# A conformer block on one core: chunk transposes by VectorE and DMA, and part of the exponentials' products on GpSimd

## Chip, cores and metric

The kernel runs on one core of a Trainium2 chip. The metric is the device time of one execution in microseconds (us); shorter is better. The engines are named as in the profile: PE (TensorE), PEld (its weight loads), DVE (VectorE), ACT (ScalarE), POOL (GpSimd) and SP (SyncE, which here issues transfers).

## What is computed

One conformer block on x of 2 x 4000 tokens with 144 features, in bfloat16: half a feed-forward layer, attention with 4 heads of 36 features over all 4000 tokens of a sequence, a gated convolution of width 5 over time, half a feed-forward layer, and a layer norm. Cut to what matters:

```python
h = layernorm(x); x = x + 0.5 * (silu(h @ w_ff1a) @ w_ff1b)
q, k, v = split(layernorm(x) @ w_qkv)
p = softmax(q @ k.T * Dh ** -0.5)            # per head: 4000 x 4000 scores
x = x + (p @ v) @ w_o
a, b = split(layernorm(x) @ w_pw1); h = a * sigmoid(b)
x = x + silu(depthwise_conv5(h, dw)) @ w_pw2
h = layernorm(x); x = x + 0.5 * (silu(h @ w_ff2a) @ w_ff2b)
return layernorm(x)
```

## The kernel before

**Chunks and score tiles.** The 8000 tokens are 16 chunks of 500 (8 a sequence), each kept as 4 blocks of 125 tokens, one token per partition. For attention, the keys of a sequence are 62 tiles of 64 and one of 32, so there are 16 x 63 = 1008 score tiles: 64 keys by 500 queries by 4 heads, as 128 partitions by 1000 columns. A tile is made by `emit_S` (L1357): four matmuls on quarters of PE's array into two PSUM banks. Its exponential goes into a slot of PT, of which there are 11, and `emit_O` (L1439) multiplies it with V by four more quarter matmuls into two banks that a chunk keeps for itself.

**Two ways to an exponential.** ACT's way (`emit_exp`, L1371) is one instruction of 1000 columns. DVE's way (`dve_tile`, L1385) has five. Two read the scores from PSUM, one per bank, and write them as 16-bit integers to a slot z. The third takes z's mantissa bits into a second slot y. The fourth (L1409) multiplies z with y into y, and the fifth keeps of z the exponent bits alone, in place. Then both y and z are multiplied with V, so a DVE tile costs PE a second product. The function `due` (L1611) says when a tile takes DVE's way; it takes 167 of the 1008 so.

**Around attention.** A chunk's normalised rows have to lie with features on partitions before a matmul can take them. `ln` (L704) does the norm: the statistics on DVE, the power -1/2 on POOL, and the rows by POOL (L724), or in the first and the last part of the kernel by DVE or ACT. `transp` (L693) then transposes the chunk: for each half of 72 features and each of the 4 blocks one PE transpose against an identity into a bank, 8 in all, and one copy of 1000 columns from PSUM to XT or XTQ. This is done five times for a chunk: ahead of the first feed-forward layer, ahead of the projections to Q, K and V (into XTQ, `ln_trq`, L756), for the attention's result AN (`post1`, L1089, written by `epilogue`, L1292), for the norm behind it, and ahead of the second feed-forward layer (`post2`, L1214). The matmuls that read XT or XTQ (`mm2`, L783, `ff_tile`, L793, `proj`, L882, `glu`, L1022) take two halves of 72 features each.

**Order of the work.** All instructions of an engine run in one order that a planner writes when the kernel is built. `Rec.op` (L71) keeps for each engine the time at which it comes free, by a cost for each instruction; `Sched` (L259) holds threads of work (`pre`, `post1`, `post2` for a chunk), and `pick_any` (L1524) chooses the next step among score tiles, exponentials, products with V and threads. A table POLICY (L373) gives 49 sections of the kernel their own parameters, AHEAD for one: how far ahead of ACT PE is to be kept. Where an instruction needs another engine's result, it waits on that engine's semaphore, and whatever stands behind it on its own engine waits too. The phase in which the first 8 chunks are prepared is called front, the one after the last exponential tail. In these two a chunk is handled in halves of two blocks.

**Start.** L568 to L597 issue the loads of x and the weights (SP and ACT) and the zeroings (POOL and DVE). DVE makes IDF, a 32-bit copy of the identity, there (L597), ahead of the first chunk's statistics.

Of the kernel before, what the change touches and what calls it, by code (L numbers as in the profile page):

```python
# [12 lines left out]
D = 144  # L13
# [29 lines left out]
def c_act(n):  # L43
    return n / 1200 + 0.051
# [6 lines left out]
class Rec:  # L51
# [6 lines left out]
    SWITCH = 0.095  # L58
# [12 lines left out]
    def op(self, eng, name, *a, r=(), w=(), q=None, cost=0.1, kind=None, lat=None, **k):  # L71
# [29 lines left out]
        if eng == "pe":  # L101
            if kind != self.kind:
                start += self.SWITCH
            self.kind = kind
# [4 lines left out]
        self.ops.append(o)  # L109
        return o  # L110
# [141 lines left out]
class Thread:  # L252
    def __init__(self, gen, ready, rank, no=0):
        self.no = no
        self.gen, self.ready, self.live, self.rank = gen, ready, True, rank
        self.req = None
# [67 lines left out]
def bass_standalone__conformer_family_zipformer__speech_kernel(  # L324
# [28 lines left out]
    def sb(name, shape, dt=BF16):  # L353
# [5 lines left out]
    NAN = 5  # L359
    TJ = (  # L360
        0.0, -0.6, 0, 0.0, -0.3, 0.0, 0.0, 0.0, 0.0, -0.6, 0.15, 0.15, -0.6, 0.0, 0.15, 0,
        0.0, 0.0, 0.0, 0.0, 0.0, 0.0, 0.3, 0.6, 0.6, -0.3, -0.3, 0.0, 0.0, 0.0, 0.0, 0.0,
        0.0, 0.0, 0.0, 0.15, 0.0, 0.0, 0.0, -0.15, 0.0, 0.0, 0.0, 0.0, 0, 0.6, 0.0, 0.0,
    )
    FJ = (
        0.0, 0.0, 0.0, 0.0, 0.0, 0.0, 0.0, 0.0, 0.0, 0.0, 0.0, 0.0, 0.0, 0.0, 0.0, 0.0,
        0.0, 0.0, 0.0, 0.0, 0.0, 0.0, 0.0, 0.0, 0.0, 0.0, 0.0, 0.0, 0, 0.0, 0.0, 0.0,
        -0.25, 0.0, 0.0, 0.0, 0.0, 0.0, 0.0, 0.0, 0.0, 0.0, 0, 0.0, 0.0, 0.0, 0.0, 0.0,
        0.0, 0.0, 0.0, 0.0, 0.0, 0.0, 0.0, 0.0, 0.0, 0.0, 0.0, 0.0, 0.0, 0.0, 0.0, 0.0,
    )  # L370
    FLEX = 0.3
    SEG = 21
    POLICY = {  # L373
        "AHEAD": (
            0.56, 0.56, 0.56, 0.85, 0.85, 0.85, 0.56, 0.56, 0.56, 0.56, 0.56, 0.56, 1.0, 1.0, 0.56, 0.56,
            0.56, 0.56, 0.56, 0.56, 0.56, 0.56, 0.56, 0.56, 0.56, 0.6, 0.6, 0.5, 0.5, 0.5, 0.5, 0.56,
            0.56, 0.56, 0.56, 0.56, 0.56, 0.56, 0.56, 0.56, 0.5, 0.5, 0.56, 0.56, 0.56, 0.56, 0.56, 0.56,
            0.56,
        ),
        "DSLACK": (  # L380
            0.4, 0.4, 0.4, 2.5, 1.5, 1.5, 1.5, 1.0, 1.0, 1.5, 0.8, 0.4, 0.4, 0.4, 0.2, 0.2,
            0.4, 0.4, 0.4, 0.4, 1.5, 1.5, 1.5, 1.5, 4.0, 4.0, 4.0, 0.4, 0.4, 0.2, 0.4, 0.4,
            0.4, 0.4, 0.4, 0.4, 0.4, 0.4, 0.2, 0.2, 0.2, 0.4, 0.4, 0.4, 0.4, 1.5, 1.5, 1.5,
            1.5,
        ),
        "DGAP": (
            2.0, 2.0, 4.0, 3.5, 4.5, 4.5, 4.5, 2.5, 2.5, 2.5, 2.5, 2.5, 2.5, 2.5, 2.5, 2.5,
            2.5, 2.5, 2.5, 2.5, 4.5, 2.5, 2.5, 2.5, 2.5, 2.5, 3.0, 3.25, 3.25, 3.0, 6.0, 3.25,
            3.25, 3.25, 3.25, 3.25, 4.0, 2.5, 2.5, 2.5, 3.25, 3.25, 3.25, 4.5, 4.5, 4.5, 3.25, 3.25,
            3.25,  # L390
        ),
        "OFREE": (
            3, 3, 1, 1, 4, 4, 1, 1, 1, 3, 0, 0, 0, 0, 1, 1,
            1, 1, 1, 1, 1, 1, 1, 1, 1, 1, 1, 2, 1, 1, 1, 1,
            1, 1, 1, 1, 1, 1, 0, 0, 0, 0, 0, 1, 2, 0, 0, 1,
            1,
        ),
        "OBATCH": (
            1, 1, 2, 1, 1, 1, 1, 1, 1, 1, 1, 1, 1, 1, 1, 1,
            1, 1, 1, 1, 1, 1, 1, 1, 0, 2, 2, 2, 2, 2, 2, 1,  # L400
            1, 1, 1, 1, 1, 1, 2, 1, 1, 1, 1, 1, 1, 1, 3, 2,
# [3 lines left out]
            0.3, 0.3, 0.3, 0.3, 0.6, 0.6, 0.1, 0.2, 0.2, 0.2, 0.2, 0.2, 0.6, 0.6, 0.6, 0.1,  # L405
            0.1, 0.1, 0.1, 0.1, 0.1, 0.3, 0.3, 0.3, 0.3, 0.3, 0.2, 0.2, 0.2, 0.3, 0.3, 0.3,
            0.3, 0.3, 0.2, 0.2, 0.2, 0.2, 0.2, 0.2, 0.2, 0.2, 0.2, 0.2, 0.2, 0.2, 0.2, 0.2,
# [3 lines left out]
            1.8, 1.8, 1.6, 1.6, 1.6, 1.6, 1.6, 2.0, 2.5, 2.5, 2.5, 2.5, 2.5, 1.4, 2.5, 2.5,  # L411
            2.5, 1.8, 2.5, 2.5, 2.5, 1.6, 1.6, 1.6, 1.6, 1.6, 1.6, 1.4, 1.4, 1.4, 1.4, 3.5,
            3.5, 3.5, 3.5, 2.5, 2.5, 1.4, 1.4, 1.4, 1.6, 1.6, 3.0, 3.0, 1.4, 1.4, 1.4, 1.8,
# [3 lines left out]
            2, 2, 2, 2, 2, 2, 2, 2, 2, 3, 3, 3, 3, 3, 2, 2,  # L417
            5, 5, 4, 2, 2, 3, 2, 2, 2, 2, 2, 2, 2, 4, 2, 4,
            4, 5, 5, 2, 2, 2, 4, 5, 5, 5, 5, 5, 5, 5, 5, 4,
# [3 lines left out]
            3, 3, 2, 2, 1, 1, 1, 1, 1, 2, 2, 2, 2, 3, 3, 3,  # L423
            3, 2, 2, 2, 2, 3, 3, 2, 2, 1, 1, 2, 2, 3, 3, 3,
            3, 3, 3, 3, 3, 3, 2, 3, 3, 4, 3, 3, 3, 3, 3, 3,
            3,
        ),
        "MAXQ": (
            2, 2, 3, 3, 1, 1, 3, 2, 1, 1, 1, 1, 1, 1, 3, 2,
            3, 3, 2, 2, 1, 2, 2, 2, 2, 1, 1, 2, 2, 2, 2, 2,  # L430
            2, 2, 2, 2, 2, 2, 3, 1, 1, 1, 3, 3, 3, 3, 3, 3,
            3,
        ),
        "EARLY": (
            2, 2, 2, 1, 3, 3, 2, 2, 2, 2, 2, 2, 2, 1, 1, 1,
            2, 2, 1, 1, 2, 2, 2, 2, 2, 2, 2, 2, 2, 2, 2, 2,
            2, 1, 1, 2, 2, 2, 3, 3, 3, 3, 3, 3, 2, 2, 2, 2,
# [3 lines left out]
            0.12, 0.12, 0.12, 0.12, 0.05, 0.05, 0.3, 0.12, 0.12, 0.05, 0.05, 0.05, 0.05, 0.05, 0.12, 0.12,  # L441
            0.12, 0.12, 0.12, 0.12, 0.12, 0.12, 0.12, 0.12, 0.12, 0.12, 0.12, 0.12, 0.2, 0.2, 0.2, 0.12,
            0.3, 0.2, 0.2, 0.2, 0.2, 0.2, 0.12, 0.12, 0.12, 0.12, 0.12, 0.12, 0.12, 0.12, 0.12, 0.12,
            0.12,
        ),
        "TWIN": (
            0.1, 0.1, 0.1, 0.1, 0.1, 0.1, 0.1, 0.1, 0.1, 0.1, 0.1, 0.1, 0.1, 0.1, 0.1, 0.1,
            0.1, 0.1, 0.1, 0.1, 0.1, 0.1, 0.1, 0.1, 0.0, 0.0, 0.0, 0.1, 0.1, 0.1, 0.1, 0.1,
            0.1, 0.1, 0.1, 0.1, 0.1, 0.1, 0.1, 0.1, 0.1, 0.1, 0.1, 0.1, 0.1, 0.1, 0.1, 0.1,
            0.1,  # L450
        ),
        "BGPICK": (
            0, 0, 0, 0, 0, 0, 0, 0, 0, 0, 0, 0, 0, 0, 0, 0,
            0, 0, 0, 0, 0, 0, 0, 0, 0, 0, 0, 0, 0, 0, 0, 0,
            1, 1, 1, 0, 0, 0, 1, 0, 0, 0, 0, 0, 0, 0, 0, 0,
# [3 lines left out]
            2, 2, 2, 1, 2, 2, 2, 2, 2, 0, 0, 0, 0, 0, 2, 2,  # L459
            2, 2, 2, 2, 2, 2, 2, 2, 2, 2, 2, 2, 2, 2, 0, 0,  # L460
            2, 2, 2, 2, 2, 3, 2, 2, 2, 2, 2, 2, 2, 2, 2, 2,
            2,
        ),
        "FDVE": (
            5, 5, 5, 5, 5, 5, 5, 5, 5, 5, 5, 5, 4, 4, 4, 5,
            5, 3, 3, 3, 3, 5, 5, 5, 5, 5, 5, 5, 5, 2, 2, 5,
            5, 5, 5, 5, 5, 5, 5, 5, 5, 5, 5, 5, 5, 1, 5, 5,
            5,
        ),
        "PRELAG": (  # L470
            0.7, 0.7, 0.7, 0.7, 0.7, 1.0, 0.7, 1.5, 1.5, 0.7, 0.7, 0.7, 0.7, 0.7, 0.7, 0.7,
            0.7, 0.7, 0.7, 0.7, 0.7, 0.7, 0.7, 0.7, 0.7, 0.7, 0.7, 1.0, 1.0, 1.0, 1.0, 0.7,
            0.7, 0.5, 0.5, 0.5, 0.5, 0.5, 0.7, 0.3, 0.3, 0.3, 0.7, 0.7, 0.5, 0.5, 0.5, 0.5,
            1.0,
        ),
        "LAGD": (
            1, 1, 1, 1, 1, 1, 1, 0, 0, 0, 0, 0, 1, 1, 0, 1,
            1, 1, 1, 1, 1, 1, 1, 1, 1, 1, 1, 1, 1, 0, 0, 0,
            1, 1, 1, 1, 1, 1, 1, 1, 1, 1, 1, 0, 0, 0, 0, 1,
# [19 lines left out]
    XN = sb("XN", [NXN, NB, D])  # L499
# [4 lines left out]
    XT = sb("XT", [NXT, 2, CW])  # L504
# [11 lines left out]
    AN = sb("AN", [NAN, NB, D])  # L516
# [24 lines left out]

    PS = nc.alloc_psum_tensor("PS", [128, 8 * 512], F32)
# [14 lines left out]

    def load_x(eng, c, r=()):
        load(eng, f"x{c}", X[0:TB, c * NB:(c + 1) * NB, :], x_tok[c], [("X", c, i) for i in range(NB)], r, 2.9)

    def load_ff(eng, qa, qb, WA, WE, WB, wa, wb, nm, la=None, lb=None):
        load(eng, qa, WA[0:HD, :, :], kh(wa)[:, :, 0:512], [(nm, "a", 0)], lat=la)
        load(eng, qa, WE[0:HD, :, 64:128], kh(wa)[:, :, 512:FF], [(nm, "a", 1)], lat=la)
        load(eng, qb, WB[:, 0:4, :], wb[0:512, :].rearrange("(t p) d -> p t d", p=128), [(nm, "b", 0)], lat=lb)
        load(eng, qb, WB[0:64, 4, :], wb[512:FF, :], [(nm, "b", 1)], lat=lb)
        load(eng, qb, WB[64:128, 5, :], wb[512:FF, :], [(nm, "b", 2)], lat=lb)

    load_x("sp", 0)  # L568
# [7 lines left out]
    op("pool", "memset", NHALF[:, :], -0.5, w=["NHALF"])  # L576
    op("pool", "memset", WP2Z[:, :, :], 0.0, w=[("WP2Z", i) for i in range(NB)], cost=0.3)
    op("pool", "memset", U2[:, :, :], 0.0, w=["U20"], cost=0.6)
    load("sp", "w2", WO[0:HD, :, :], kh(w_o), ["WO"])
    load("sp", "w2", WP1[0:HD, :, :], kh(w_pw1), ["WP1"])  # L580
# [9 lines left out]
    for WE, WB, nm, eng in ((WE1, WB1, "W1", "dve"), (WE2, WB2, "W2", "pool")):  # L590
        op(eng, "memset", WE[0:HD, :, 0:64], 0.0, w=[(nm, "a", 2)], cost=0.15)
        op(eng, "memset", WE[0:HD, :, 128:192], 0.0, w=[(nm, "a", 3)], cost=0.15)
# [61 lines left out]
    def setup_dw():  # L654
        for ab in range(2):
            op("dve", "tensor_copy", WPZ[0:HD, :, 48 + 64 * ab:64 + 64 * ab], WP1[0:HD, :, ab * D + ML:(ab + 1) * D],
               r=["WP1", "WPZ0"], w=["WPZ"], cost=0.15)
# [35 lines left out]
    def transp(src, rk, dst, wk, n, rows=TB):  # L693
# [830 lines left out]
    def pick_any():  # L1524
# [46 lines left out]
        if n_s[0] >= NIT and o:  # L1571
            return o[0]
# [133 lines left out]
```

## Time and profile before

| | |
|---|---|
| Median of 3 runs | 914.84 us (914.69 to 915.0) |
| The profiled execution: its own time, its span | 914.9 us, 913.1 us |
| Granted TensorE clock | 0.999 |
| Busy: PE, DVE, ACT, POOL | 890.1, 802.0, 872.9, 277.5 us |
| First exponential, last exponential start | 20.59 us, 877.89 us |
| Exponentials on ACT | 825 of 1000 columns, 16 of 500 |
| Normalisations of a block on POOL | 224, mean 599 ns |
| Transfers | 7.36 MB in 7322 packets |

The span runs from the first to the last instruction of the profiled execution; the time is a little longer. A group line gives line, engine, operation, out<-in by the program's names, shapes (partitions x elements), count, then busy time and the mean in ns of one, then the idle time of the engine just before them and who ended it. Nearly every instruction has line 170, since one helper (`replay`) issues them all, so groups are told apart by names and shapes. A line of a stretch gives, after its bounds and length, the busy time (and count) of PE, PEld, DVE, ACT and POOL, the granted clock, and the share and rate of the DMA engines. A line of the timeline gives start, duration, engine, line, operation, names and count.

### The profile page before, as it was taken

What the parts mean: (1) busy time and instruction counts of PE and PEld (TensorE: products, weight loads), DVE (VectorE), ACT (ScalarE), POOL (GpSimd) and SP (SyncE); (2) the same over time, 40 slices, a digit from 0 to 9 for tenths busy, and PEclk for the clock granted to TensorE, in tenths of its full rate; (3) what the DMA queues carried; (4) which work ended last, traced back from release to release, by engine and by line L of the source; (5) the groups of instructions that cost most, each with busy time, mean ns of one, the idle gap of its engine ahead of it and who ended that gap; (6) DMA issues with size and microseconds to landing.
All of it is one profiled execution on the core that took longest, in us unless ns stands there. A gap on an engine that the chain in (4) does not pass through costs nothing.

```text
span 913.1 us, 27439 instructions
## 1 busy us (share of the span) xinstructions
PE 890.1 (97%) x11946; PEld 411.2 (45%) x11946; DVE 802.0 (88%) x1756; ACT 872.9 (96%) x1105; POOL 277.5 (30%) x519
## 2 busy tenths in 40 slices
PE   8999999999999999999999999999999999999996
PEld 7544434444444444444444444444434344444455
DVE  8988898898989999898988799897889699978987
ACT  5899999999999999999999999999999999999984
POOL 5121041145111612223415333240605050403143
PEclk9999999999999999999999999999999999999999
DMA  4000000000000000000000000000000000000000
GB/s 114 34 2 1 2 2 1 1 3 1 3 3 1 3 2 2 2 3 1 2 2 14 1 9 8 8 2 1 15 1 2 8 9 2 8 1 8 2 8 26
DMA packets 7322, 7.36 MB, mean 8 GB/s; under 512 B 2376, under 2 KB 7202, under 8 KB 7202
## 3 DMA queue, kind: packets, MB, share of 16 engines
q1 hardware_dynamic: 5786, 5.00, 1.8%
q8 instruction: 93, 1.52, 0.7%
q10 hardware_dynamic: 1416, 0.62, 0.3%
q14 instruction: 27, 0.22, 0.1%
HBM read 3.31 MB, written 2.30 MB: 6 GB/s over the span
## 4 chain that ended last, share of the span: by engine, by line
ACT 51%; PE 43%; DVE 4%; issue 1%; DMA 0%; POOL 0%; POOLq 0%; DVEq 0%
ACT PT L170 46%; PE PS L170 43%; ACT TH L170 5%; DVE HT L170 1%; DVE PT L170 1%; DVE ST L170 1%; DMA X<-in_x_dram 0%; DVE X L170 0%; DVE XN L170 0%; DVE QT L170 0%; POOL RS L170 0%; DVE XT L170 0%; DVE RS L170 0%; DVE SW L170 0%; DVE VA L170 0%
## 5 line engine op out<-in xcount | busy, mean ns | idle before, releaser
L170 ACT ACTIVATE PT<-PS 128x1000 bf16<-128x1000 f32 (+1 forms) x841 | 777.2, 1050 | 8.3 <-PE PS L170 5.9
L170 PE MATMUL PS<-QT,KT 64*64 64x500 bf16 x3968 | 415.6, 383 | 8.6 <-ACT PT L170 5.6
L170 PE MATMUL PS<-PT,VA 64*37 64x500 bf16 x4636 | 396.1, 373 | 1.9 <-DVE QT L170 1.4
L170 DVE TENSOR_SCALAR PT<-PS 128x500 int16<-128x500 f32 x334 | 222.4, 671 | 31.5 <-PE PS L170 29.5
L170 PEld LDWEIGHTS PS<-QT,KT 64*64 64x64 bf16 x3968 | 123.8, 104 | 195.7 <-ACT PT L170 112.5
L170 PEld LDWEIGHTS PS<-PT,VA 64*37 64x37 bf16 x4636 | 132.1, 95 | 111.3 <-issue 26.7
L170 POOL TENSOR_SCALAR RS<-ST 125x4 f32<-125x4 f32 x112 | 36.6, 327 | 471.0 <-DVE ST L170 465.8
L170 DVE TENSOR_SCALAR PT<-PT 128x1000 uint16<-128x1000 uint16 x334 | 134.7, 416 | 1.3
L170 POOL TENSOR_SCALAR XN<-X,RS 125x144 bf16<-125x144 bf16 x224 | 131.8, 599 | 5.8
L170 POOL TENSOR_TENSOR RS<-RS,NHALF 125x4 f32<-125x4 f32 (+2 forms) x101 | 94.1, 936 | 101.6 <-DVE RS L170 96.9
L170 DVE TENSOR_TENSOR PT<-PT 128x1000 bf16<-128x1000 bf16 x167 | 113.0, 681 | 1.5
L170 ACT ACTIVATE TH<-PS 128x500 bf16<-128x500 f32 (+3 forms) x198 | 104.3, 552 | 6.7 <-PE PS L170 5.6
L170 DVE SCALAR_TENSOR_TENSOR HT<-TH,PS 128x500 bf16<-128x500 bf16 (+1 forms) x135 | 80.6, 616 | 25.1 <-ACT TH L170 24.4
L170 PE MATMUL PS<-XT,WA 72*128 72x500 bf16 (+2 forms) x280 | 74.3, 360 | 0.6 <-DVE VA L170 0.3
L170 DVE SCALAR_TENSOR_TENSOR X<-PS,X 125x288 bf16<-125x288 f32 x128 | 57.4, 452 | 14.8 <-PE PS L170 13.1
L170 DVE BATCH_NORM_STATS2 ST<-X 125x6 f32<-125x288 bf16 (+1 forms) x160 | 65.8, 447 | 1.0 <-DMA X<-in_x_dram 0.8
L170 PE MATMUL PS<-WB,HT 128*125 128x144 bf16 (+1 forms) x640 | 52.7, 230 | 0.3 <-DVE HT L170 0.3
L170 PEld LDWEIGHTS PS<-WB,HT 128*125 128x125 bf16 (+1 forms) x640 | 44.3, 136 | 14.8 <-issue 3.8
L170 PE MATMUL PS<-IDENT,XN 125*72 125x125 bf16 x512 | 42.4, 221 | 1.5 <-DVE XN L170 0.9
L170 DVE COPY XT<-PS 72x1000 bf16<-72x1000 bf16 (+2 forms) x65 | 39.9, 617 | 3.3 <-PE PS L170 2.5
L170 PEld LDWEIGHTS PS<-IDENT,XN 125*72 125x72 bf16 x512 | 31.5, 112 | 20.2 <-issue 12.6
L170 PE MATMUL PS<-U,DG 128*128 128x250 bf16 (+5 forms) x204 | 34.3, 265 | 0.1
(86 smaller groups left out, 560.6 us busy)
## 6 DMA issues: line engine op xcount, KB each, us to landing
X<-in_x_dram SPq DMA_DIRECT2D x16, 140.6 KB
out_dram<-XN SPq DMA_DIRECT2D x14, 140.6 KB
WA<-in_w_ff1a_dram ACTq DMA_DIRECT2D x1, 144.0 KB
WB<-in_w_ff1b_dram ACTq DMA_DIRECT2D x1, 144.0 KB, 2.6
WA<-in_w_ff2a_dram SPq DMA_DIRECT2D x1, 144.0 KB
WB<-in_w_ff2b_dram SPq DMA_DIRECT2D x1, 144.0 KB
out_dram<-XN SPq DMA_DIRECT2D x2, 70.3 KB
WQKV<-in_w_qkv_dram ACTq DMA_DIRECT2D x1, 121.5 KB
```

Of the source, the lines that this page charges most:

```text
L170: ins = getattr(eng, o.name)(*o.a, **o.k)
```

## The change

**Products.** In `dve_tile`, the fourth instruction goes to POOL when POOL will, by the planner's clock, be free before DVE plus an allowance PTS, and not in the front. The words of the change say that this holds for 109 of 192 DVE tiles.

```diff
-        yield need("dve")
-        op("dve", "tensor_tensor", yf, zf, yf, op=ALU.mult, r=[("PT", z), ("PT", y)], w=[("PT", y)],
-           cost=c_dve(2 * CH, 2), kind="e")
+        pool = not mode["front"] and R.free["pool"] < R.free["dve"] + now("PTS")
+        yield need("pool" if pool else "dve")
+        op("pool" if pool else "dve", "tensor_tensor", yf, zf, yf, op=ALU.mult, r=[("PT", z), ("PT", y)], w=[("PT", y)],
+           cost=G_COST if pool else c_dve(2 * CH, 2), kind="e")
...
+    G_COST = 2.3
```

**Transposes.** Outside front and tail, the rows of two blocks are interleaved, element by element, so that two bfloat16 make one 32-bit word. One DVE instruction transposes the tile's 32 x 32 blocks of words in place, four transfers on SP write it to a tensor in DRAM, and two more read it back as XT (128 and 16 features) or XTQ (72 and 72). The matmuls that read XT take it with a column step of two, and the output's columns in the order of the blocks. In front and tail PE transposes as before, but in parts of 128 and 80 rows, with a copy for each.

```diff
+    def blocks(v, key, z, reads, q, wk):
+        yield need("dve")
+        op("dve", "transpose", v, v, r=[key], w=[key], cost=c_dve(320))
+        yield need("sp")
+        first, v = None, v.rearrange("p (g k n) -> p g k n", g=2, n=32)
+        for a in range(4):
+            args = "sp", "dma_start", DR[z, :, :, a, :, :].rearrange("k r g n -> r g k n"), v[32 * a:32 * a + 32, :, :, :]
...
+        for dst, f0, f1, n in reads:
+            args = "sp", "dma_start", dst, d[f0:f1, :, :, :].rearrange("f g a n -> f g (a n)")[:, :, 0:n]
...
+        if dma:
+            yield from blocks((ANF if an else XNF)[:, u, :], key, s,
+                              [(XTF[0:128, s, 0, :, :], 0, 128, 128), (XTF[0:16, s, 1, :, :], 128, D, 128)], f"t{s}", wk)
+            return
...
+        for k in range(2):
+            yield need(eng, hold=True)
+            copy(XT[0:kr[k], s, k, bs[0]:bs[-1] + 1, 0:rows], ps[0:kr[k], k, :, 0:rows], [("ps", bk)], wk, n * rows, 2.0,
+                 eng)
...
+    SP_COST = 0.36
+    W_LAT = 2.0
+    T_LAT = 2.4
```

**Weights and start.** The weights that XT meets are split in 128 and 16 rows, the second part padded with zeros to 80. For that, and since the interleaved tiles are wider than what is written of them, more is zeroed at the start, and each such weight takes one transfer more:

```diff
+    zero_k("dve", WA1, ("W1", "z", 0))
+    zero_e("dve", WE1, "W1")
+    op("dve", "memset", XNS[:, :, :], 0.0, w=[("XN", u) for u in range(NXN)], cost=0.9)
+    op("dve", "memset", XT[0:LP, :, 1, :, :], 0.0, w=[("XT", u, i) for u in range(NXT) for i in range(NB)], cost=0.75)
...
+    zero_k("pool", WO, "WOZ")
+    zero_k("pool", WP1, "WP1Z", 0.25)
+    zero_k("pool", WA2, ("W2", "z", 0), 0.4)
+    zero_e("pool", WE2, "W2")
     op("pool", "memset", WP2Z[:, :, :], 0.0, w=[("WP2Z", i) for i in range(NB)], cost=0.3)
+    op("pool", "memset", ANS[:, :, :], 0.0, w=[("AN", a) for a in range(NAN)], cost=1.6)
...
-        op(eng, "memset", WE[0:HD, :, 0:64], 0.0, w=[(nm, "a", 2)], cost=0.15)
-        op(eng, "memset", WE[0:HD, :, 128:192], 0.0, w=[(nm, "a", 3)], cost=0.15)
```

**Plan.** AN has 4 buffers, not 5. The planner's costs change: `c_act` from 0.051 to 0.053, SWITCH from 0.095 to 0.094, a normalisation on POOL from 0.65 to 0.45 with 0.8 more for the first, and PE gets bubbles at some switches (`bub`). Nearly all entries of POLICY are new, with three new rows: PTS (above), BURST and BAGE. These two hold back PE's other work while little of it is ready and none of it has waited long:

```diff
+        if ok and R.kind == "q" and (s or o) and sum(q[2].req.dur for q in ok) < now("BURST") and min(
+                q[2].since for q in ok) > R.free["pe"] - now("BAGE"):
+            ok = []
```

## The prediction

> **What bounds the kernel now.** I read the page's first two parts, then the stretches of the span, then the chain of waits, then the groups with their forms kept apart.
>
> ```profile
> span 913.1 us, 27439 instructions
> PE 890.1 (97%) x11946; PEld 411.2 (45%) x11946; DVE 802.0 (88%) x1756; ACT 872.9 (96%) x1105; POOL 277.5 (30%) x519
> ACT 51%; PE 43%; DVE 4%; issue 1%; DMA 0%; POOL 0%; POOLq 0%; DVEq 0%
> ```
>
> PE's 97% is modelled, so it proves little; ACT's 96% is made of whole instructions. The chain runs by turns on ACT and PE. The stretches tell which of them is full (PE, PEld, DVE, ACT, POOL in that order, us busy):
>
> ```profile
> 0.00:26.00 26.00, 23.16 (x285) 17.56 (x286) 21.54 (x78) 16.41 (x30) 12.38 (x30) 1.00 0.41 115
> 26.00:100.00 74.00, 72.46 (x920) 35.25 (x918) 62.44 (x164) 67.20 (x96) 12.69 (x19) 1.00 0.02 7
> 100.00:800.00 700.00, 690.96 (x9416) 303.55 (x9414) 626.62 (x1292) 693.17 (x848) 221.05 (x411) 1.00 0.01 4
> 800.00:890.00 90.00, 87.78 (x1140) 40.96 (x1134) 74.69 (x164) 85.82 (x112) 23.83 (x50) 1.00 0.02 5
> 890.00:913.10 23.10, 15.69 (x198) 13.86 (x195) 16.73 (x62) 10.28 (x25) 7.55 (x10) 0.94 0.09 26
> ```
>
> From 100 to 800 us ACT rests 6.8 us of 700: one percent. DVE rests 73.4 us there, 10.5%. **ACT is the bound**, and what it executes is mostly exponentials. The prices of a tile are in these groups:
>
> ```profile
> L170 ACT ACTIVATE PT<-PS 128x1000 bf16<-128x1000 f32 x825 | 768.8, 1057 | 7.8 <-PE PS L170 5.4
> L170 DVE TENSOR_SCALAR PT<-PS 128x500 int16<-128x500 f32 x334 | 222.4, 671 | 31.5 <-PE PS L170 29.5
> L170 DVE TENSOR_SCALAR PT<-PT 128x1000 uint16<-128x1000 uint16 x334 | 134.7, 416 | 1.3
> L170 DVE TENSOR_TENSOR PT<-PT 128x1000 bf16<-128x1000 bf16 x167 | 113.0, 681 | 1.5
> L170 DVE COPY XT<-PS 72x1000 bf16<-72x1000 bf16 x51 | 34.3, 673 | 3.1 <-PE PS L170 2.4
> ```
>
> There are 16 x 63 = 1008 score tiles: 167 by DVE's five instructions, 841 by ACT (825 whole, 16 half).
>
> **The change, part by part.** The working is against the profiled execution: 914.9 us, span 913.1 and 1.8 around it; the median of the runs is 914.84, the same.
>
> *More tiles leave ACT.* The change's words give 192 DVE tiles, so 25 more. ACT loses 25 x 1.057 = **26.4 us** (872.9 to 846.5). As ACT is 99% busy in the stretch where nearly all these tiles lie, that is the gain if PE and DVE follow. The nearest limits: none of it, if they don't.
>
> *PE.* Chunk transposes: 60 copies of the 1000-wide form (51 plus one on ACT for XT, 8 for XTQ) each stand for 8 PE transposes 55 ns apart. Two lie past the last exponential (877.9 us), where they stay, so 58 x 8 x 0.055 = 25.5 us of PE goes, and the changes to and from score matmuls around them. Added: 25 tiles bring one more product with V each, 4 matmuls at the 52 ns pace of four, 25 x 4 x 0.0525 = 5.3 us. PE is eased by 20 us or more, about as much as ACT, so it doesn't become the bound.
>
> *DVE.* 25 more tiles at 2 x 0.671 + 2 x 0.416 + 0.681 = 2.86 us: +71.4. 109 products gone to POOL at 0.681: -74.2. 58 copies at 0.673 become block transposes of 128x320 words, a form the trace lacks: between DVE's 250-wide (0.41) and 500-wide (0.67) forms on words from PSUM, 0.48 as the nearer; 58 x (0.48 - 0.673) = -11.2 (bounds -15 and 0). Zeroing and split copies: +5. Sum 802.0 - 9 = **793**, without waits on POOL.
>
> *POOL.* The product there has no row. By bounds: the zeroing of 128x640 takes 0.64 us (1 ns an element), a normalisation of 144 elements 0.459 us where nothing disturbs it and a copy of 2 elements 0.257, 1.4 ns an element; one operand more doubles that at most. So 1.0 to 3.0 us; I take 2.2 and 109 x 2.2 = 240, POOL at 517 us of some 890: it fits. The Trainium skill (GPSIMD Engine Reference, section 3.1) has 4497 ns for a sum of 2048 float elements; an estimate from it is 2.2 us; no run here shows it.
>
> *What POOL does to DVE.* This speaks against the change. DVE's uint16 PT instructions start inside a POOL instruction 117 times. Read one by one, where they start over 0.08 us into an undisturbed normalisation, they end 0.27 us after it ends (or at their own 0.41, if that is later); where they come first, the normalisation waits and takes 0.77 us on average:
>
> ```profile
> 587.19 0.65 DVE L170 TENSOR_SCALAR PT<-PT 128x1000 uint16<-128x1000 uint16 x1
> 586.66 1.50 POOL L170 TENSOR_SCALAR XN<-X,RS 125x144 bf16<-125x144 bf16 x3
> 1.53 2.53 DVE L170 CAST IDF<-IDENT 128x128 f32<-128x128 bf16 x1
> 1.45 0.58 POOL L170 MEMSET WP2Z<- 128x576 bf16 x1
> 3.45 0.52 POOL L170 MEMSET WK<- 128x512 bf16 x1
> ```
>
> 0.65 in place of 0.41 us; and the small cast waits out POOL's whole row of zeroings, 1.45 to 3.97. Evacuations from PSUM (0.671) are the same beside POOL or not, and POOL's power instruction (1.04 us on 4 elements) holds nobody. The Trainium skill (SBUF — State Buffer, Who interferes with whom) says so too: a VectorE instruction that uses two ports or has two SBUF inputs shares a port pair with GpSimd, and whichever starts second waits for the whole of the other. The trace agrees for the rows above, not for the power instruction. By that sentence a product would block DVE for up to its 2.2 us.
>
> How often? In before I laid a window of 2.2 us from the start of each of the 167 products and looked for another tile's in-place instruction in it (the own tile's last step waits for the product anyway): 29% have one, which would wait 0.71 us on average: 0.2 us a product, 109 x 0.2 = 22 us on DVE. Bounds: 0, and 2.2 - 0.14 = 2.06 us a product. Behind the waiting instruction stand DVE's evacuations, then PE's banks, then ACT. DVE's 73 us of rest take the 22; the plan lets PE run some 0.6 us ahead of ACT (AHEAD), so 32 meetings cost ACT about 0.1 each: **+3.5** (bounds 0 and 22).
>
> *The transposes' way through DRAM.* Latency grows from some 1.5 us to 0.48 + 6 issues x 0.36 + 2.0 + 2.4 = 7 us, by the plan's own terms. Issues in the trace take 0.26 to 0.55 us on SP; the one small SBUF to SBUF transfer lands in 1.7 us, weights in 2.6 to 2.8. Cover: chunks are prepared tens of us ahead and SP idles from 25 us on. 58 x 6 issues x 0.36 = 125 us of SP: fits. Output stores queue behind a waiting transfer, and nobody waits for those before the end. Cost 0; without cover, rival 3. Fewer AN buffers: as much, nothing.
>
> *Front.* POOL gets zeroings of 144, 288, 512, 64, 256 and 2560 columns and loses one pair: at 0.9 ns a column (start to start in the row above) +3.15 us. The cast of IDF stands ahead of the first statistics on DVE and waits them out: statistics start at about 7.2, not 4.84 us: **+2.4** on the chain to the first exponential (bounds 0, 3.2). *Tail:* the last chunk's transposes get two copies in place of one, 3 x 0.15: **+0.5**. Other edits (the plan's cost figures, order tables) only move instructions.
>
> **Sum:** 914.9 - 26.4 + 3.5 + 2.4 + 0.5 = **894.9 us**.
>
> **Rivals.**
> 1. *Forecast*, ACT still the bound: 883 to 906. Chance 0.58.
> 2. *Better packing*: the new plan also takes the 11 us that ACT rests in 26:100 and 800:890, and hides the 3.5: 880. For it: PE is eased by more than ACT there. Against: work of the first chunks waits for its own results. 0.10.
> 3. *Transfers land later than the plan allows.* PE takes its instructions in order, so the first matmul that reads such a tile holds up the score matmuls behind it: 58 x 0.5 us = 29, 924. Against: the trace's landings are near the plan's. 0.06 (half of that or of rival 4, 906 to 913: 0.08).
> 4. *DVE becomes the bound, slower*: POOL's products hold DVE. DVE's rest outside 100:800 is 37.6 us, so DVE's end stands at 793 + 37.6 + waits. It passes ACT's 887 from 0.5 us a product and the old span from 0.75 us; at 0.9 it is 929 us. For it: more tiles live at once than in before, so more meetings than 29%. 0.13.
> 5. *No change* (913 to 917): rivals 3 and 4 at some 0.6 of their price, or fewer tiles leave ACT than the words say: 0.05, of which 0.04 within 0.2%.
>
> A run here can tell about 0.2% from no change. Faster by more: 0.58 + 0.10 + 0.08 = 0.76; within: 0.04; slower: 0.06 + 0.13 + 0.01 = 0.20. Range for 8 in 10: it leaves out the best packing (under 876, 0.06) and the dearer half of rivals 3 and 4 (over 920, 0.14): 876 to 920.
>
> **What the profile after would show.** ACT's PT group at 800 of 1000 wide, ACT over 98% busy in the middle. DVE's in-place uint16 instructions with a mean of 0.45 to 0.5, not 0.416; a mean over 0.8 is rival 4, and DVE then rests under 3% in the middle. PE waiting on DMA for XT in more than a few places is rival 3. The cast of IDF at some 2.5 us or more and the first exponential at 23, not 20.6 us, show the front. POOL's products at 2.2 us; under 1.5 or over 3 moves the waits with them. Wrong altogether if the middle of ACT falls under 96%.

## The result, and the profile after

The kernel after takes 976.03 us in the median of 4 runs (974.31 to 976.69), the kernel before 914.82 beside it: a ratio of 1.0666, 95% interval 1.0648 to 1.0685. It is slower by 61 us, where 20 us less was forecast. The profiled execution took 976.69 us.

The page of the kernel after: its head, and the shares of the chain of waits.

```profile
span 974.8 us, 27315 instructions
PE 897.1 (92%) x11622; PEld 394.1 (40%) x11622; DVE 853.2 (88%) x1788; ACT 866.5 (89%) x1098; POOL 502.2 (52%) x634
...
PE 45%; DVE 36%; ACT 13%; DMA 3%; SPq 2%; issue 1%; POOL 0%; POOLq 0%; DVEq 0%
```

No engine is as full now as ACT was. ACT was 51% of the chain and is 13%; DVE was 4% and is 36%. The stretch from 100 to 800 us of the kernel after, columns as before:

```profile
100.00:800.00 700.00, 648.56 (x8403) 263.52 (x8396) 608.73 (x1196) 639.49 (x770) 384.82 (x469) 0.99 0.12 26
```

ACT rests 60.5 us there, before 6.8. DVE, which the chain names so often, rests *more* there than before: 91.3 us, not 73.4. So DVE isn't short of time; its results come late. The groups, forms kept apart, say which:

```profile
L181 ACT ACTIVATE PT<-PS 128x1000 bf16<-128x1000 f32 x800 | 756.1, 1021 | 71.0 <-PE PS L181 66.1
L181 DVE TENSOR_SCALAR PT<-PS 128x500 int16<-128x500 f32 x384 | 254.7, 669 | 29.1 <-PE PS L181 27.4
L181 DVE TENSOR_SCALAR PT<-PT 128x1000 uint16<-128x1000 uint16 x384 | 220.3, 588 | 4.5 <-POOL PT L181 2.8
L181 DVE STREAM_TRANSPOSE XN<-XN 128x320 f32<-128x320 f32 x44 | 21.9, 498 | 0.0
L181 POOL TENSOR_TENSOR PT<-PT 128x1000 bf16<-128x1000 bf16 x109 | 230.3, 2114 | 221.1 <-DVE PT L181 221.1
```

The uint16 steps have a mean of 0.588 us, before 0.416. Read one by one, 67 of them start inside a product on POOL and take 1.41 us on average, 1.0 more than their own 0.41: 67 us in all. The other 317 take 0.41. Of the 109 products 64 lengthen a step of DVE (62 of these steps and two of DVE's own two-operand products), by 1.06 us each. DVE's steps that read PSUM stay at 0.669. The view of waits passes it on (us in all, times, longest):

```profile
PEld PS L181 <- DVE PT L181: 146.4, 301, 2.1
ACT PT L181 <- PE PS L181: 66.5, 100, 2.9
PEld PS L181 <- DMA XTQ<-rows: 7.3, 4, 2.5
PE PS L181 <- DMA XTQ<-rows: 5.8, 4, 2.2
```

In before the first of these was 61.5 us and the second 5.9. How one product does it is seen in the timeline of the kernel after around 400 us, engine by engine (start, duration):

```profile
400.20 2.07 POOL L181 TENSOR_TENSOR PT<-PT 128x1000 bf16<-128x1000 bf16 x1 [1.54 <-DVE PT L181]
...
400.62 1.92 DVE L181 TENSOR_SCALAR PT<-PT 128x1000 uint16<-128x1000 uint16 x1
402.47 0.67 DVE L181 TENSOR_SCALAR QT<-PS 128x500 bf16<-128x500 f32 x1
...
402.60 0.60 PE L181 MATMUL PS<-PT,VA 64*37 64x500 bf16 x6 [1.13 <-DVE PT L181]
...
403.47 2.79 ACT L181 ACTIVATE PT<-PS 128x1000 bf16<-128x1000 f32 x3 [1.05 <-PE PS L181]
```

The product runs from 400.20 to 402.27. DVE's uint16 step starts at 400.62 and ends at 402.54, 0.27 us after it. The product with V that needs it stands ahead of score matmuls on PE, which idles 1.13 us; then ACT idles 1.05. The step shows as busy time of DVE: the wait is inside it, and no view of idle time has it.

### The profile page after: what moved, and what is told of

Its sections match the earlier page's. It is cut to its first block, busy times and chain, and to the rows that moved or that the text cites. A ratio compares the mean times of both kernels' runs of the same rounds, so it can differ in the third digit from the quotient of the medians.

```text
span 974.8 us, 27315 instructions
## 1 busy us (share of the span) xinstructions
PE 897.1 (92%) x11622; PEld 394.1 (40%) x11622; DVE 853.2 (88%) x1788; ACT 866.5 (89%) x1098; POOL 502.2 (52%) x634
## 4 chain that ended last, share of the span: by engine, by line
PE 45%; DVE 36%; ACT 13%; DMA 3%; SPq 2%; issue 1%; POOL 0%; POOLq 0%; DVEq 0%
PE PS L181 45%; DVE PT L181 24%; ACT PT L181 11%; ACT TH L181 2%; DVE HT L181 2%; SPq L181 2%; DVE QT L181 2%; DVE ST L181 1%; DVE X L181 1%; DVE XN L181 1%; DMA XTQ<-rows 1%; DVE AN L181 1%; DMA rows<-XN 1%; DVE KT L181 1%; DVE VA L181 0%
## 5 line engine op out<-in xcount | busy, mean ns | idle before, releaser
L181 ACT ACTIVATE PT<-PS 128x1000 bf16<-128x1000 f32 x816 | 764.5, 1013 | 71.4 <-PE PS L181 66.5
L181 PE MATMUL PS<-PT,VA 64*37 64x500 bf16 x4736 | 435.0, 378 | 36.0 <-DVE PT L181 33.2
L181 PE MATMUL PS<-QT,KT 64*64 64x500 bf16 x3968 | 428.9, 384 | 21.4 <-DVE PT L181 8.2
L181 POOL TENSOR_TENSOR PT<-PT 128x1000 bf16<-128x1000 bf16 x109 | 230.3, 2114 | 221.1 <-DVE PT L181 221.1
L181 DVE TENSOR_SCALAR PT<-PS 128x500 int16<-128x500 f32 x384 | 254.7, 669 | 29.1 <-PE PS L181 27.4
L181 DVE TENSOR_SCALAR PT<-PT 128x1000 uint16<-128x1000 uint16 x384 | 220.3, 588 | 4.5 <-POOL PT L181 2.8
L181 PE MATMUL PS<-XT,WA 128*128 128x500 bf16 (+5 forms) x288 | 77.2, 365 | 1.9 <-DMA XT<-rows 1.3
L181 DVE TENSOR_TENSOR PT<-PT 128x1000 bf16<-128x1000 bf16 x83 | 58.6, 707 | 0.9
L181 PEld LDWEIGHTS PS<-XT,WA 128*128 128x128 bf16 (+1 forms) x288 | 20.0, 98 | 36.2 <-issue 12.2
L181 DVE COPY QT<-PS 128x1000 f32<-128x1000 f32 (+1 forms) x16 | 18.7, 1167 | 10.8 <-PE PS L181 10.6
```

The source lines that it names most:

```text
L181: ins = getattr(eng, o.name)(*o.a, **o.k)
```

## The experiments

Theory A: a POOL product keeps DVE's in-place steps waiting, and the waits reach the end nearly whole. Rival B: the transposes' round trips through DRAM come late. Rival C: the new order itself packs worse. All ratios are to the kernel before, with 95% intervals.

**One part undone, planner run anew.** Products all on DVE (821 tiles for ACT, 187 for DVE came out):

```diff
-        pool = not mode["front"] and R.free["pool"] < R.free["dve"] + now("PTS")
+        pool = False
```

> The changed kernel with every product on DVE again, planned anew by its own planner (821 tiles on ACT, 187 on DVE, transposes through DRAM kept). Theory A (POOL's products hold up DVE's in-place steps, 67 us in the changed kernel, and these waits pass on to PE and ACT): the uint16 steps fall back to a mean of 0.41 us and the time to 890-915 us. Theory B (transposes that land later than planned hold up PE): the cause stays, 940-975 us. Theory C (the new order packs PE and ACT worse in itself): 940-975 us.

Measured: 956.39 us, 1.0441 (1.0412 to 1.0471). The uint16 steps are at 0.415, so the holding is gone, but not the loss. PE's loads now wait 23.0 us for XT from DRAM (16 times, up to 4.2 us), where they waited 2.7 in the kernel after, and 52 us pass from the last exponential's start to the end, where 37.5 did. The table of the plan was made for another distribution, so this run changes the order, the transfers and the tail at once. It misses A's figure and lies in the range named for B and C, but it doesn't decide between them.

The product in four pieces of 250 columns:

```diff
-        op("pool" if pool else "dve", "tensor_tensor", yf, zf, yf, op=ALU.mult, ...)
+            for c0 in range(0, 2 * CH, 250):
+                args = "pool", "tensor_tensor", yf[:, c0:c0 + 250], zf[:, c0:c0 + 250], yf[:, c0:c0 + 250]
```

> The changed kernel, each of the 109 products on POOL issued as four of 250 columns one behind the other, same planned cost. Theory A: a step of DVE that meets a product waits for a quarter of it at most (0.5 us, mean 0.25 in place of 1.06, if DVE comes in between two), so DVE's waits fall from 67 to some 20 us and the time to 920-940 us. If DVE can't come in between, 976 or more. Theories B and C: 970-985 us.

Measured: 939.86 us, 1.0286 (1.0246 to 1.0326). The four pieces take 2.8 us together (0.704 each), more than the 2.11 of one, and yet 36 us are won: a step waits for the end of a piece, no longer of the product. 110 steps wait 0.27 us each, 30 us in all. Had a product's own length been the cost, this had been slower.

Transposes back on PE, products on POOL as in the change (108 of 183 tiles):

```diff
-        inter = len(bs) == NB and not calm()
+        inter = False
... (the same in `ln_trq` and for AN in `epilogue`)
```

> The changed kernel with all chunk transposes on PE as in its front and tail, planned anew, products on POOL kept (108 of 183). Theory A: still slow, 950-985 us, uint16 steps at a mean near 0.58 us. Theory B: the waits for transfers go, 915-935 us. Theory C: near 976 us.

Measured: 988.09 us, 1.0799 (1.0782 to 1.0815). Without any round trip it is slower still, above every figure named; its uint16 steps wait 56 us inside products. This speaks against B as the main cause. It is no proof, as the order is a new one here too (48.6 us from the last exponential's start to the end); what B costs is measured further down.

The kernel before with POOL products alone (107 of 168 tiles):

```diff
+        pool = not mode["front"] and R.free["pool"] < R.free["dve"] + 0.5
-        yield need("dve")
-        op("dve", "tensor_tensor", ...)
+        yield need("pool" if pool else "dve")
+        op("pool" if pool else "dve", "tensor_tensor", ...)
```

> The kernel before with nothing new but the rule that gives a product to POOL when it is free (allowance 0.5 us; 107 of 168), planned anew. Theory A: slower than before, by 40 to 70 us: 955-985 us, uint16 steps near 0.58 us. Theories B and C: within some 10 us of 914.8 us.

Measured: 963.24 us, 1.0536 (1.0519 to 1.0554). 45 steps wait 0.78 us each inside products, 35 us. But 51.5 us pass from its last exponential's start to the end, 35.2 in before: an order written anew has a cost of its own, as in the first run of this row. A lower granted clock is not needed for the loss: this kernel was granted 0.999, as before was, and the kernel after 0.987.

**Orders held fixed.** So in all later runs the instruction order of a kernel was kept, and its list of instructions was edited behind the planner. First, in the order after, each POOL product gives way to a POOL instruction that is as long and, by the prediction's reading, holds nobody, the power on 10 columns:

```diff
+    for k, o in enumerate(prods):
+        o.a = (PW[:, 2 + k % 4, :], PW[:, 0, :], PW[:, 1, :])
+        o.k = dict(op=ALU.pow)
...
```

> The changed kernel in its own order, instruction for instruction, but for one thing: each of the 109 products on POOL is replaced by a power instruction on 10 elements of a scratch tile, sized to last about 2.1 us too (the power instruction on 4 elements held nobody in the profile of before). Left out: the 109 products themselves. All waits on POOL's result stay, its hold on DVE goes. Theory A: DVE's uint16 steps at 0.41-0.43 us, 67 us of waits gone, and they pass on nearly whole: 905-925 us. Theory B or C, or if the product's latency is what costs: 955-976 us.

Measured: 918.22 us, 1.0046 (1.0022 to 1.0069).

```profile
L181 DVE TENSOR_SCALAR PT<-PT 128x1000 uint16<-128x1000 uint16 x384 | 153.9, 415 | 3.6 <-POOL PWR L181 1.8
```

Whoever waited for POOL's product now waits for a power of 2.0 us, and the uint16 steps are free. Of 61 us of loss 58 are gone. Next, the products left out altogether:

```diff
+    gone = set(map(id, prods))
+    R.ops = [o for o in R.ops if id(o) not in gone]
+    for o in R.ops:
+        o.deps = [d for d in o.deps if id(d[0]) not in gone]
```

> The changed kernel in its own order with the 109 products on POOL left out and nothing in their place: neither hold nor latency. Theory A: within 10 us of e5_latency_no_hold, 900-915 us; what then still lies over the 887 us of ACT's work belongs to the front and to transfers (B) or to the order (C).

Measured: 923.08 us, 1.0092 (1.0061 to 1.0124), above the 900 to 915 that was named, and no faster than with the powers (whose ten runs spread from 914.54 us to 923.91). So in this order the time that a product takes on POOL costs nothing that shows; that it holds DVE costs 53 us (to this run) to 58 (to the one ahead), for 67 us of waits.

The same products moved to DVE, in the same places:

```diff
+    for o in prods:
+        o.eng = "dve"
```

> The changed kernel in its own order, the 109 products executed by DVE at the place where POOL got them: no hold, but 109 x 0.67 = 73 us of work that the order did not allow DVE. Theory A in the stricter form (any lateness of DVE passes on one to one): like the changed kernel, 955-985 us. If only the hold on both engines costs, 910-930 us.

Measured: 949.73 us, 1.0382 (1.0365 to 1.0398), between the two figures named. DVE's products take 72.8 us more than the 83 alone (129.8 against 57.0), and as neighbours overlap, DVE is busy for 57.0 us more in all (845.2 against 788.2). That cost 27 us: 0.37 to 0.47 a microsecond, against 0.8 to 0.9 for the waits. VectorE doing the whole product itself is cheaper than POOL doing it. DVE's rest over the whole span, 131.1 us without products, took 26 of this work (104.8 left), and only 10 of the waits (121.5 left in the kernel after); why the two differ was not tested.

**The same price in the order of before.** To shut out the new order, 109 products on a scratch row were added to the kernel before, in the places of DVE's own, which stay; and in a second kernel 109 powers:

```diff
+            e.name, e.a, e.k = "tensor_tensor", (SCR[:, 0, :], SCR[:, 0, :], SCR[:, 0, :]), dict(op=ALU.mult)
...
+            e.deps = [(d, True) for d in R.hist["SCR"][0]] + [(d, True) for d, raw in o.deps if d.eng == "dve" and raw]
```

> The order of the kernel before, instruction by instruction, with 109 added GpSimd products on a scratch row that nobody reads (750 columns, by the rows of 1000 and of 250 columns about 1.6 us each), each let go by what lets VectorE's own product of that tile go. VectorE still does all of its work. Theory A (GpSimd's products hold VectorE's in-place steps, and a wait in an order written out by hand is passed on nearly whole): VectorE's uint16 steps wait some 30 to 60 us in all, and the time is 940 to 965. Rival C (what was lost belongs to the order and the tables of the kernel after, or to VectorE's rest being too small there; in the order of before, with 73 us of rest in the middle, the waits are taken up): 915 to 922.

Measured: 970.12 us, 1.0602 (1.0586 to 1.0618): slower than A's upper end. Groups and stretch of this kernel:

```profile
L170 POOL TENSOR_TENSOR SCR<-SCR 128x750 bf16<-128x750 bf16 x109 | 178.1, 1634 | 259.8 <-DVE PT L170 258.8
...
L170 DVE TENSOR_SCALAR PT<-PT 128x1000 uint16<-128x1000 uint16 x334 | 162.9, 500 | 1.3
L170 DVE TENSOR_TENSOR PT<-PT 128x1000 bf16<-128x1000 bf16 x167 | 148.1, 890 | 1.6
```

```profile
100.00:800.00 700.00, 660.03 (x8797) 281.88 (x8799) 632.64 (x1205) 657.78 (x793) 354.83 (x474) 0.99 0.01 4
```

> As the kernel with 109 added products, in the same places, but each added instruction is a GpSimd power over 10 columns, which lasts about as long (2.0 us). Theory A: no step of VectorE is held, uint16 steps stay at 0.41 us wherever they fall, time 913 to 920. Were it only GpSimd's queue (its later instructions coming late) that costs, this kernel would be as slow as the one with the added products.

Measured: 926.30 us, 1.0118 (1.0101 to 1.0135).

```profile
L170 DVE TENSOR_SCALAR PT<-PT 128x1000 uint16<-128x1000 uint16 x334 | 134.7, 416 | 1.3
L170 DVE TENSOR_TENSOR PT<-PT 128x1000 bf16<-128x1000 bf16 x167 | 113.2, 681 | 1.5
```

Nobody reads the added results. With the products DVE's two in-place groups grow by 28.2 and 35.1 us over before (134.7 and 113.0), 63 us, and the time by 55. With the powers they don't grow, and the time grows by 11, more than expected. In the profiled execution, 14.4 us longer than before, 8.0 of these lie behind the last exponential's start (43.2 us, in before 35.2), and from 300 to 350 us ACT rests 5.8 us, in before 0.5. POOL's own rows XN, RS and PW are 3% of the chain, so its later work probably comes late; that part was not tested by itself. Between the two, which differ in the added operation and by 0.5 us in its length: 44 us. And DVE still rests 67.4 us from 100 to 800 with the products, 73.4 in before. **The waits did not go into the rest.**

**What was left without the holding.** In the run without products ACT rests 27.8 us between 100 and 800, and 11.4 of these in one place. Its stretch, and its chain of waits (start, duration):

```profile
150.00:200.00 50.00, 44.19 (x500) 18.32 (x498) 34.10 (x71) 38.59 (x47) 12.02 (x23) 0.87 0.17 37
```

```profile
167.25 0.62 SPq L181
167.87 0.04 issue
167.91 0.61 SPq L181
168.52 0.04 issue
168.56 3.12 DMA rows<-XN
171.68 0.02 issue
171.70 0.89 SPq L181
172.59 0.04 issue
172.63 2.47 DMA XTQ<-rows
175.10 0.05 issue
175.15 0.61 PE PS L181 x2
```

From the first store's issue (166.62 by the timeline of SP) to PE's matmul 8.5 us pass. To take the store's landing out, the loads were let read rows of x:

```diff
-        first, d = None, DR[z, :, :, :, :, :].rearrange("k r a g n -> (k r) g a n")
+        first, d = None, XR[z, :, :, :, :, :].rearrange("k r a g n -> (k r) g a n")
...
+    for o in loads:
+        o.deps = [d for d in o.deps if not (d[0].eng == "sp" and d[0].q is not None and d[0].q[0] == "d")]
```

> The order of the kernel after with the 109 GpSimd products left out, as in the run before of that kind (923.1), and besides each load of a DRAM transpose reads rows of the input x in the place of the rows just stored, so that it waits for no store to land; the stores are still issued. The output is not the reference's (the products and the right rows are left out). Theory B (the round trips through DRAM come later than planned, PE and ACT stand still for them between 150 and 400 us): the rests of ACT between 100 and 400 us fall from some 22 us to under 10 and the time to 903 to 912. Rival C (the order itself holds less work beside ACT there): 918 to 925.

Measured: 912.43 us, 0.9973 (0.9962 to 0.9983), 10.7 us less than with the wait for the stores. The same stretch of this kernel, then its middle:

```profile
150.00:200.00 50.00, 46.92 (x613) 20.05 (x610) 39.87 (x84) 44.89 (x55) 16.06 (x32) 0.97 0.17 38
```

```profile
100.00:800.00 700.00, 681.09 (x9018) 285.20 (x9014) 602.44 (x1286) 679.66 (x830) 203.12 (x402) 0.99 0.13 28
```

ACT gets 6.3 us back in that one stretch. So B is true, at some 11 us, just above its own figure and below C's. This is the price of the stores' landings alone, as the loads still travel. Part of it goes with the clock: where both kernels were granted 0.994, one run took 919.6 us and three took 912.7 on average, 7 us apart; whether the waits lowered the clock was not tested. The expectation named 10 us of rest; between 100 and 400 ACT still rests 14.7 us, most of it at 150 to 200 and 300 to 350, and the cause of these two was not taken apart.

**The front.** In the order after, the cast of IDF was put behind the 60th activation:

```diff
+    cast = next(o for o in R.ops if o.eng == "dve" and o.name == "tensor_copy")
+    R.ops.remove(cast)
...
+    R.ops.insert(at, cast)
```

> The changed kernel with one instruction moved: the cast of IDF leaves its place ahead of the first statistics on DVE and comes behind ACT's sixtieth instruction. The front's part of the cause: first exponential at 20.8-21.2 in place of 23.4 us; time 2-3 us shorter, 973-974 us, if the front is on the chain to the end; unchanged if not.

Measured: 971.98 us, 1.0620 (1.0602 to 1.0637), a little below the 973 to 974 named, but not by the front: the first exponential starts at 23.17 us and not at 21, since POOL's power still stands behind its own zeroings (7.21 us, 7.48 in the kernel after). The 4 us that were won lie in the middle (ACT rests 56.9 us there in place of 60.5), not in the front, and what won them is open. On top of the run without round trips, POOL's zeroing of AN was moved behind the second power as well:

```diff
+    z = next(o for o in R.ops if o.eng == "pool" and o.name == "memset" and tuple(o.a[0].shape)[1:] == (NAN, 640))
+    R.ops.remove(z)
...
+    R.ops.insert(at + 1, z)
```

> As the run without round trips, and besides the cast of the identity on VectorE comes after the 60th activation and GpSimd's zeroing of AN after its second power instruction. Theory: the first exponential starts at 21.0 to 22.0 us and not at 23.4, and the time is 1.5 to 2.5 us below that run's; if the front is nothing to the end, the same as that run's.

Measured: 911.98 us, 0.9967 (0.9955 to 0.9979), the same as that run within the runs' spread, and the first exponential at 23.45. The timeline of this kernel (POOL, then DVE) shows why:

```profile
7.15 2.23 POOL L181 MEMSET AN<- 128x2560 bf16 x1
...
6.57 2.91 DVE L181 TENSOR_SCALAR XN<-X,ST,RS 125x144 bf16<-125x144 bf16 x4 [0.69 <-POOL RS L181]
9.46 0.20 DVE L181 MEMSET WPZ<- 128x176 uint32 x1
```

The power now comes at 5.82 us, as in before. But the zeroing, at its new place, meets DVE's normalisations: four take 2.91 us where they took 1.22 in the kernel after (two of them last 2.20 and 2.00 us and not 0.31), and they end at 9.48, where the kernel after ended them at 9.45. The wait was moved, not removed.

No run with the whole computation beat the kernel before. Even with the products and the waits for the stores taken out, the order after is only 0.3% faster than before, so these runs point to no version of the change that would be.

## Why the prediction was wrong, step by step

- **The step that failed:** "DVE's 73 us of rest take the 22; [...] so 32 meetings cost ACT about 0.1 each: +3.5 (bounds 0 and 22)". The mechanism was named and found; that DVE's rest would swallow it was wrong. The rest is not a store of time: it lies in pieces between instructions whose order is fixed, and a late result passes through PE's order to ACT. The added products in before show it without the new order: 63 us of waits, 55 us of time, DVE's rest down by 6. In the kernel after 67 us of waits cost 53 to 58. The rest is not useless: with the products moved to DVE it took 26 of 57 us of work. Of the waits, which the forecast gave to it nearly whole, it took 10.
- *How often.* 29% of the windows were forecast to hold another in-place step; 64 of 109 products, 59%, lengthened one. The count was taken in the order of before, with a window as long as the product. The new order has 25 more such tiles, and its planner books a product on POOL without closing DVE meanwhile; that this doubles the share was not tried.
- *How long.* 0.71 us each forecast, 1.06 measured. Together 0.62 us a product, where 0.2 was said: 67 us on DVE, not 22. The sentence of the Trainium skill (SBUF — State Buffer, Who interferes with whom), that the second waits for the whole of the other, was weighed there and its result kept as a bound; the steps read one by one obey it for the products.
- *Rival 4* had the mechanism and put its price by DVE's end, 793 + 37.6 + waits. With 67 us that is 898, under the old span, and the kernel took 976. DVE never became full: it rests 13% from 100 to 800 us, where under 3% was the sign of it, and the uint16 mean of 0.588 lies between the 0.45 to 0.5 of the forecast and the 0.8 of this rival. The sign of being wrong altogether was met: ACT is busy for 91% of the middle, under 96%.
- *Round trips: cost 0.* Measured 10.7 us for the stores' landings alone. Landings were as planned in the median (2.0 us), but stores are issued in 0.62 us each, not 0.36, and the last landing in the chain shown took 3.12; 8.5 us in place of 6.5. Rival 3's mechanism is right, at a third of its price, and in a few places.
- *ACT: -26.4.* A mean of 1.057 us counts the overlap of neighbours twice: the group's busy time is 768.8 for 825, 0.932 each, 23.3 for 25. Of ACT's work 846.5 us was forecast, and 857.8 measured without products: 15.1 us less than before, not 26.4. There the 800 whole ones took 0.938 each of the group's busy time (750.5), and the rest of the difference was not taken apart.
- *Right:* POOL's product (2.2 forecast, 2.11; luck in part, as the rows gave only bounds of 1.0 and 3.0, with the second operand's price taken on trust), the block transpose (0.48, 0.498), the first exponential (23, 23.42), DVE's work without waits (793 with 83 products; 788.2). The cost of the front could not be taken back by either edit. The tail came out at 37.5 us behind the last exponential's start, 35.2 in before: +2.3, not +0.5.
- *The sum again.* The span is ACT's busy time and its rest, so the profiled executions add up on ACT: before, 872.9 + 40.2 = 913.1; without products and without the waits for stores, 857.0 + 54.1 = 911.1; without products, 857.8 + 61.5 = 919.3; the kernel after, 866.5 + 108.3 = 974.8. So the tiles that left ACT took 15.9 us of work from it, and 13.9 more of rest ate nearly all of that. The stores' landings add 8.2 and the products 55.5 (10.7 and 52.9 by the medians). What part of the 13.9 belongs to the new order itself, to the front (2.8 us later) or to the loads that still travel was not settled.

## What to carry to other kernels

Work given to an idle GpSimd was paid here by VectorE wherever the two met on 16-bit steps from and to SBUF, so look in the trace for steps whose own duration grows, as idle time does not show such waits; a power that lasts as long and holds nobody, put in the product's place, tells holding from lateness in one run. An engine's rest in a fixed order is not free time (here it took 26 of 57 us of work moved to DVE, and 10 of 67 us of waits): price a wait by what stands behind it on that engine and on the next, and try it by adding idle instructions to the kernel that exists, with its order kept. Moving a step and letting the planner run anew changes everything at once and settles little.

## What the runs showed of the hardware

- *Who waits.* In the kernel after, beside POOL's products, only DVE's 16-bit steps in SBUF grew: uint16 steps 1.41 us on average (67) against 0.41. Steps from PSUM (70, 0.670 against 0.669), the statistics (15, 0.442 against a median of 0.446) and the block transposes of 32-bit words (11, 0.496 against a median of 0.500) did not, though the last two read SBUF. In the kernel before with products on a scratch row, 49 of DVE's own two-operand products started inside and took 1.39 us against 0.68.
- *When they are let go.* The uint16 steps end 0.28 us behind POOL's product in the median, DVE's two-operand products 0.54.
- *The power is another thing.* In the kernel before with added powers, 104 uint16 steps and 60 products of DVE started inside POOL powers of 2.16 us; the longest took 0.427 and 0.683. The Trainium skill (SBUF — State Buffer, Who interferes with whom) lets whichever starts first keep the shared ports for its whole instruction; that holds for the products here and not for the power.
- *POOL's product* of two bfloat16 rows took 2.11 us for 1000 columns, 1.63 for 750 and 0.70 for 250 (in the run in pieces).
- *Zeroing holds too:* in the last run, beside the zeroing of AN (7.15 to 9.38 us), two of four normalisations on DVE ended only 0.1 us behind it, and the four took 2.91 us in place of 1.22.
- *Granted clock:* where PE stood still for transfers (150 to 200 us without products), it was 0.87, and 0.97 with the waits for the stores gone. The run of the kernel with powers that took 914.54 us was granted 0.996, the one of 923.91 us 0.987.
